# The last layer's softplus: second sum on VectorE, later steps, six buffers; first half part's sums copied by VectorE

## The chip, the cores and the metric

The kernel runs on one core of one Trainium2 chip. The metric is the time of one execution in device microseconds (us); the table below gives the median of three runs and one profiled execution. The engines are named as in the profile: PE (matmul) and PEld (its weight loads), DVE (VectorE), ACT (ScalarE), POOL (GpSimd), SP (the queue that issues most transfers).

## The reference, cut to what matters

Causal attention with a cumulative bias (2 batches, 8 heads, 576 tokens, head size 64) gives 1152 tokens of width 512. A mixture of eight experts follows, whose gate is normalised by rows and columns eight times. The last layer is a plain two-matmul block whose activation is softplus:

```python
def _moe2_ref(x, w_in, w_out) -> np.ndarray:
    h = x @ w_in                                     # 1152 x 512 by 512 x 2048
    g = np.maximum(h, 0.0) + np.log1p(np.exp(-np.abs(h)))
    return (g @ w_out).astype(np.float32)            # 1152 x 2048 by 2048 x 512
```

## The kernel before, in words

Attention comes first. Then 20 "half parts" `x` run one after the other, each with 512 columns of a hidden layer: 16 for the eight experts (`x < NX`, NX = 16), and four for the last layer (x = 16 to 19). Every float32 operand is split into its highest bits (`hh`, `w1h`, `xh`; type fp32r) and the rest (`hl`, `w1l`, `xl`), so that one product takes three matmuls.

Each half part has two stages of PE work, and the hand-written order mixes the second stage of one half part with the first stage of the next:

- First stage in the last layer, `plain` (line 340). A unit is 128 hidden columns by 288 tokens. It takes twelve matmuls into one bank `ph` and is played as two steps `p` of six matmuls. There are sixteen units for each half part, eight for tokens 0 to 575 (`g` = 0) and eight for tokens 576 to 1151 (`g` = 1).
- After each unit `evict` (line 230) makes softplus from the bank. ACT takes the absolute value, its exponential and log1p (lines 250 to 252, tiles `a1` and `a3`). `sums` puts four instructions into the queues: DVE computes 1 + a1 - 1 (line 256) and max(h, 0) + a3 (line 257), which is the bank's last reader; POOL computes a1 less that rounded value (line 258, into `a2`) and adds it to `a3` (line 259). `high` then rounds `a3` to `hh` on ACT (line 262), and `rest_` subtracts it on DVE, giving `hl` (line 265). The three tiles come from the pool `m3`, four buffers each.
- Second stage, `downs` (line 359). For a tile `t` of 128 tokens it adds four steps `d` of three matmuls into a bank `py`, which read `hh`, `hl` and the output weights `w2h`, `w2l`. After the fourth step `total` (line 382) takes the bank into `acc`: ACT copies it for the first half part of either layer (x = 0 and x = 16, line 385), and DVE adds it otherwise (line 388, or line 391 with the gate). There are two `py` banks, `y1` and `y2`, used in turn, so the first matmul of a tile waits for the `total` of the tile two before it.

The engines' queues keep the order in which the program issues instructions. `defer(k, step)` sets when a step is issued: `flush()` is called once for every `p` and every `d`, and a step deferred with `k` is issued at the flush numbered k + 1 after it. So `sums`, `high` and `rest_` are issued at flush 2, 5 and 6 after the unit's end. The order of the last layer's half parts is written out by hand, `=n` and `wn` starting the splitting of the next half part's weights (ACT line 146 and DVE line 149 for `w1`; ACT line 199 and DVE or POOL line 201 for `w2`):

```python
A_PLAIN = "p p p p d d p d p d p d p d =0 p d p d p d p d p d p d p d p =1 d d d"
B_PLAIN = "d d =2 d d p p d p d p d p p d p d p d p d p d p d d w0 p d d w2 p d d w1 p d d w3 p p"
A_GROUPS = [(0, 1), (2,), (3,)]
B_GROUPS = [(4,), (5,), (6,), (7, 8)]
```

In `A_PLAIN` the `p` steps are units of the same half part with `g` = 1 and the `d` steps are tiles 0 to 3 (tiles 0 and 1 share their steps, one matmul group each in turn). In `B_PLAIN` the `d` steps are tiles 4 to 8 and the `p` steps are units of the next half part with `g` = 0. Ahead of half part 16 twelve `p` follow each other with transposes of the layer's input (`turn`, lines 899 to 921) between them, and the four `p` of `A_PLAIN` follow on those. Half part 19 ends with twenty `d` alone.

Of the kernel before, what the change touches and what calls it, by code (L numbers as in the profile page):

```python
# [14 lines left out]
ALU = mybir.AluOpType  # L15
# [5 lines left out]
def attention_moe_ffn(ctx, tc, q, k, v, s, w_gate, w1, w2, w_in, w_out, out):  # L21
    nc = tc.nc
# [11 lines left out]
    NX = w1.shape[0]  # L34
# [18 lines left out]
    def f(ap):  # L53
        return ap.bitcast(F32)
# [154 lines left out]
    m3_t = []  # L209
# [4 lines left out]
    def defer(k, x):  # L214

        late.append([k, x])
# [13 lines left out]
    def evict(x, k, z, q, cols):  # L230

        hh, hl = hb[0][:, q, cols], hb[1][:, q, cols]
        if x < NX:
            def high():
                nc.scalar.activation(out=hh, in_=z, func=AF.Relu)  # L235

            def rest_():
                nc.vector.scalar_tensor_tensor(out=hl, in0=z, scalar=0.0, in1=f(hh), op0=ALU.max, op1=ALU.subtract)  # L238

            if k < 0:  # L240
                high()
            else:
                defer(k, high)
            defer(k + 1, rest_)
            return
        m3 = m3_t[-1]
        a1 = m3.tile([P, HB], F32, tag="a1", name="a1")
        a2 = m3.tile([P, HB], F32, tag="a2", name="a2")
        a3 = m3.tile([P, HB], F32, tag="a3", name="a3")
        nc.scalar.activation(out=a1, in_=z, func=AF.Abs)  # L250
        nc.scalar.activation(out=a1, in_=a1, func=AF.Exp, scale=-1.0)  # L251
        nc.scalar.activation(out=a3, in_=a1, func=AF.Ln, bias=1.0)

        def sums():

            nc.vector.tensor_scalar(a2, a1, 1.0, -1.0, ALU.add, ALU.add)  # L256
            nc.vector.scalar_tensor_tensor(out=a3, in0=z, scalar=0.0, in1=a3, op0=ALU.max, op1=ALU.add)
            nc.gpsimd.tensor_tensor(out=a2, in0=a1, in1=a2, op=ALU.subtract)  # L258
            nc.gpsimd.tensor_tensor(out=a3, in0=a3, in1=a2, op=ALU.add)  # L259

        def high():
            nc.scalar.activation(out=hh, in_=a3, func=AF.Copy)  # L262

        def rest_():
            nc.vector.tensor_tensor(out=hl, in0=a3, in1=f(hh), op=ALU.subtract)  # L265

        defer(1, sums)
        defer(4, high)
        defer(5, rest_)

    class Unit:

# [56 lines left out]
        def p3(self):  # L329
            self.product(self.a, S4, B22, False)  # L330
            flush()
            evict(self.x, -1, self.a, self.p, self.h1)
# [26 lines left out]
    def downs(x, groups):  # L359

        for tiles in groups:
            py = {}
            for t in tiles:
                nd[0] += 1
                py[t] = ps.tile([P, DM], F32, tag=f"y{1 + nd[0] % 2}", name="py", bufs=1)
            if x == XE:
                for t in tiles:
                    a = acc[0][:, t, :]
                    nc.gpsimd.tensor_scalar(a, a, gate_t[0][:, t, 0:1], 1.0, ALU.mult, ALU.mult)
            for k, ft in enumerate((0, 2, 1, 3)):  # L370
                wh, wl = wt[x, 2, ft]
                for t in tiles:
                    tsl = slice(t * P, (t + 1) * P)
                    hh, hl = hb[0][:, ft, tsl], hb[1][:, ft, tsl]
                    for n, (u, v) in enumerate(((hh, wh), (hh, wl), (hl, wh))):
                        nc.tensor.matmul(py[t], u, v, start=(k == 0 and n == 0), stop=(k == NF - 1 and n == 2))  # L376
                    flush()
                    if k == NF - 1:
                        total(x, t, py[t])
                    yield  # L380

    def total(x, t, py):
        a = acc[0][:, t, :]
        if x == 0 or x == NX:
            nc.scalar.activation(out=a, in_=py, func=AF.Copy)
            return
        if x < XE or x > NX:
            nc.vector.tensor_tensor(out=a, in0=py, in1=a, op=ALU.add)  # L388
        else:
            e = x // XE  # L390
            nc.vector.scalar_tensor_tensor(out=a, in0=py, scalar=gate_t[0][:, t, e:e + 1], in1=a,  # L391
                                           op0=ALU.mult, op1=ALU.add)
        if x == NH - 1:
            nc.sync.dma_start(out=out[t * P:(t + 1) * P, :], in_=a)
# [3 lines left out]
    with tc.manual_schedule():  # L398
# [500 lines left out]
        def turn(g):  # L899

            h, l = (z.rearrange("p b c n -> p b (c n)") for z in (xh[g], xl[g]))
            r = slice(g * REM, (g + 1) * REM)
            t0, o0 = (NB + 1, REM) if g else (0, 0)
            o1 = 0 if g else NB * P
            px = ps.tile([P, KD, REM], F32, tag="tr", name="px", bufs=2)
            for c in range(KD):
                nc.tensor.transpose(px[:, c, :], acc[0][r, NB, c * P:(c + 1) * P], ident[r, r])
            o = slice(o1, o1 + REM)
            nc.scalar.activation(out=h[:, :KD, o], in_=px, func=AF.Copy)
            yield  # L910
            nc.vector.tensor_tensor(out=l[:, :KD, o], in0=px, in1=f(h[:, :KD, o]), op=ALU.subtract)
            yield
            o = slice(o0, o0 + NB * P)
            for c in range(KD):
                px = ps.tile([P, 512], F32, tag="tr", name="px", bufs=2)
                for t in range(NB):
                    nc.tensor.transpose(px[:, t * P:(t + 1) * P], acc[0][:, t0 + t, c * P:(c + 1) * P], ident)
                nc.scalar.activation(out=h[:, c, o], in_=px, func=AF.Copy)
                yield
                nc.vector.tensor_tensor(out=l[:, c, o], in0=px, in1=f(h[:, c, o]), op=ALU.subtract)  # L920
                yield
# [23 lines left out]
        def rest():  # L945
            for z in back:
                for _ in z:
                    pass
            back.clear()
# [3 lines left out]
        def products(x, g):  # L953

            if x < NX:
                u = dict(a=Unit(x, 0, g), b=Unit(x, 1, g))
                return {z: getattr(u[z[0]], "p" + z[1]) for z in ORDER.split()}

            def sums():
                for i in range(2):  # L960
                    for j in range(2):
                        for p in range(2):
                            yield from plain(x, p, g, i, j)

            z = sums()
            return {"p": lambda: next(z)}

        def play(seq, todo, d=None):


            for z in seq.split():
                if z[0] in "=w":
                    dense[0] = z[0] == "w"
                if z[0] == "=":
                    back.append(prep1(x + 1, int(z[1])))
                    continue
                if z[0] == "w":
                    back.append(prep2(x + 1, int(z[1])))
                    continue
                if z == "d":  # L980
                    next(d)
                else:
                    todo[z]()
                step(z)
# [8 lines left out]
        x = -1  # L993
# [4 lines left out]
        for x in range(NH):  # L998
            if x == NX - 2:
                for _ in conv:  # L1000
                    pass
                cv.close()
                m3_t.append(ctx.enter_context(tc.tile_pool(name="m3", bufs=4, reuse_waits="tile")))
            play(A_SEQ if x < NX else A_PLAIN, products(x, 1), downs(x, A_GROUPS))
            d = downs(x, B_GROUPS if x + 1 < NH else [(t,) for t in range(NB, NTT)])
            if x + 1 < NX:
                play(B_SEQ, products(x + 1, 0), d)
            elif x + 1 == NX:
                play("d d d d", {}, d)
                rest()  # L1010
                back.append(turn(0))
                for _ in range(8):
                    play("d", {}, d)
                    step()
                rest()
                u = products(NX, 0)
                play("d d w0 p d d w2 p d d w1 p d d w3 p", u, d)
                back.append(turn(1))
                play("p p p p p p p p p p p p", u)
                rest()  # L1020
            elif x + 1 < NH:
                play(B_PLAIN, products(x + 1, 0), d)
            else:
                play(" ".join("d" * 20), {}, d)
            if x == XE - 1:
                for _ in gates:
                    pass
                gt.close()
                conv = convert(cv.enter_context(tc.tile_pool(name="cv", bufs=2, reuse_waits="tile")))
# [56 lines left out]
```

## Time and profile before

| what | value |
|---|---|
| median of three runs | 1121.05 us (1119.55 to 1121.26) |
| the profiled execution's own time | 1118.75 us |
| span of the profile, first to last instruction | 1117.0 us |
| mean granted TensorE clock | 0.991 of full speed |
| busy: PE, PEld, DVE, ACT, POOL | 1080.4, 951.8, 737.8, 528.1, 419.6 us |

The profile shows one execution. The last layer's units begin about 891 us into the span and its last matmul starts at 1112.50 us. PE is busy for 97% of the whole span, so what other engines do matters only where PE stands still or runs at a lower clock.

### The profile page before, as it was taken

Reading aid. Unit: us, or ns where it says so; the run is one execution under the profiler, and the core shown is the slowest. Engines: PE = TensorE matmul, PEld = TensorE weight load, DVE = VectorE, ACT = ScalarE, POOL = GpSimd, SP = SyncE. Lnnn points to the kernel's source line nnn. Section 1 sums busy time; section 2 is a strip of 40 time slices with the busy share of each in tenths; the row PEclk is TensorE's granted clock in tenths of the full one; section 3 lists DMA queues with packets and bytes.
Section 4 is the critical chain, followed back from the end, with each engine's and each line's share of the span. In section 5 each row is a group of like instructions: output and inputs, shape, how many; then the busy total and the mean of one; then the engine's idle time right before and its main releaser. Section 6 shows DMA issues by size and latency. Waiting matters only on the chain.

```text
span 1117.0 us, 18144 instructions
## 1 busy us (share of the span) xinstructions
PE 1080.4 (97%) x6692; PEld 951.8 (85%) x6692; DVE 737.8 (66%) x1641; ACT 528.1 (47%) x1246; POOL 419.6 (38%) x493
## 2 busy tenths in 40 slices
PE   4989999999999999999999999999999999999998
PEld 3767789898988988889888898889889898888887
DVE  4456645847878778787878888775555575465553
ACT  3988644233443434334343443334334267656551
POOL 5876411134423324142341523413020065555552
PEclk9999999999999999999999999999999999999999
DMA  5222102032122322223132222311112111111001
GB/s 171 85 78 66 40 1 76 3 112 94 67 94 95 125 83 87 95 94 121 60 114 95 95 90 75 129 58 38 38 39 76 38 39 38 39 38 38 1 11 75
DMA packets 30424, 78.48 MB, mean 70 GB/s; under 512 B 6048, under 2 KB 10656, under 8 KB 30336
## 3 DMA queue, kind: packets, MB, share of 16 engines
q1 hardware_dynamic: 27768, 68.93, 19.1%
q0 software_dynamic: 2560, 8.39, 1.9%
q8 instruction: 52, 0.85, 0.3%
q14 instruction: 36, 0.29, 0.1%
q10 hardware_dynamic: 8, 0.01, 0.0%
HBM read 66.00 MB, written 10.82 MB: 69 GB/s over the span
## 4 chain that ended last, share of the span: by engine, by line
PE 82%; DVE 7%; ACT 5%; POOL 3%; issue 2%; SPq 1%; DMA 0%; POOLq 0%; DVEq 0%; ACTq 0%
PE py L376 41%; PE ph L287 31%; PE ph L351 4%; POOL a L259 2%; PE sc L551 1%; POOL a L258 1%; PE pv L665 1%; DVE a L256 1%; DVE hl L265 1%; PE tr L639 1%; ACT hh L262 1%; ACT a L251 1%; ACT eb L608 1%; PE tr L633 1%; ACT a L250 1%
## 5 line engine op out<-in xcount | busy, mean ns | idle before, releaser
L376 PE MATMUL py<-w2h,hh 128*128 128x512 f32 x720 | 287.2, 399 | 7.4 <-DVE acc L388 6.1
L376 PE MATMUL py<-w2h,hl 128*128 128x512 f32 x720 | 285.2, 396 | 1.0 <-DVE hl L238 1.0
L376 PE MATMUL py<-w2l,hh 128*128 128x512 f32 x720 | 285.2, 396 | 0.0
L287 PE MATMUL ph<-xh,w1h 128*128 128x288 f32 x896 | 265.1, 296 | 2.5 <-ACT v L295 2.5
L287 PE MATMUL ph<-xh,w1l 128*128 128x288 f32 x896 | 264.8, 296 | 0.0
L287 PE MATMUL ph<-xl,w1h 128*128 128x288 f32 x896 | 263.3, 294 | 0.0
L287 PEld LDWEIGHTS ph<-xh,w1h 128*128 128x128 f32 x896 | 167.9, 187 | 20.0 <-ACT v L295 2.8
L287 PEld LDWEIGHTS ph<-xl,w1h 128*128 128x128 f32 x896 | 168.3, 188 | 16.5
L287 PEld LDWEIGHTS ph<-xh,w1l 128*128 128x128 f32 x896 | 168.2, 188 | 0.0
L376 PEld LDWEIGHTS py<-w2h,hl 128*128 128x128 f32 x720 | 135.7, 188 | 34.1 <-DVE hl L238 1.6
L201 POOL TENSOR_TENSOR w2l<-raw,w2h 128x512 fp32r<-128x512 f32 x40 | 55.4, 1384 | 287.4 <-ACT w2h L199 287.4
L235 ACT ACTIVATE hh<-ph 128x288 fp32r<-128x288 f32 x192 | 78.8, 412 | 159.8 <-DVE ph L337 81.2
L376 PEld LDWEIGHTS py<-w2h,hh 128*128 128x128 f32 x720 | 135.5, 188 | 21.2 <-DVE acc L388 6.8
L376 PEld LDWEIGHTS py<-w2l,hh 128*128 128x128 f32 x720 | 135.9, 189 | 11.6
L295 ACT ACTIVATE v<-ph 128x288 f32<-128x288 f32 x128 | 51.0, 411 | 171.7 <-PE ph L287 164.8
L391 DVE SCALAR_TENSOR_TENSOR acc<-py,gate,acc 128x512 f32<-128x512 f32 x126 | 94.0, 746 | 54.2 <-PE py L376 54.0
L894 POOL TENSOR_TENSOR cm<-cm,ct 128x512 f32<-128x512 f32 x32 | 45.1, 1409 | 202.5 <-DVE ct L892 202.5
L238 DVE SCALAR_TENSOR_TENSOR hl<-ph,hh 128x288 fp32r<-128x288 f32 x192 | 86.7, 454 | 30.5 <-ACT hh L235 28.7
L149 DVE TENSOR_TENSOR w1l<-raw,w1h 128x512 fp32r<-128x512 f32 (+1 forms) x144 | 99.8, 694 | 8.3 <-ACT w1h L146 8.2
L265 DVE TENSOR_TENSOR hl<-a,hh 128x288 fp32r<-128x288 f32 x64 | 38.0, 594 | 71.9 <-ACT hh L262 71.9
L146 ACT ACTIVATE w1h<-raw 128x512 fp32r<-128x512 f32 (+1 forms) x144 | 82.9, 577 | 1.6 <-PE ph L287 1.6
L258 POOL TENSOR_TENSOR a<-a,a 128x288 f32<-128x288 f32 x64 | 51.8, 809 | 78.8 <-DVE a L256 61.4
(182 smaller groups left out, 1766.1 us busy)
## 6 DMA issues: line engine op xcount, KB each, us to landing
raw<-in_w SPq DMA_DIRECT2D x64, 512.0 KB
f<-in_w_in SPq DMA_DIRECT2D x16, 512.0 KB
f<-in_w_out SPq DMA_DIRECT2D x16, 512.0 KB
wd<-cm POOLq DMA_DIRECT2D x32, 256.0 KB, 3.2
raw<-wd SPq DMA_DIRECT2D x16, 512.0 KB
out<-acc SPq DMA_DIRECT2D x9, 256.0 KB
vv<-in_v SPq DMA_DIRECT2D x8, 256.0 KB
qk<-in_k SPq DMA_DIRECT2D x7, 288.0 KB
```

Of the source, the lines that this page charges most:

```text
L146: nc.scalar.activation(out=hi[:, o], in_=t[:, src], func=AF.Copy)
L149: nc.vector.tensor_tensor(out=lo[:, o], in0=t[:, src], in1=f(hi[:, o]), op=ALU.subtract)
L201: (nc.gpsimd if i else nc.vector).tensor_tensor(out=lo, in0=t[:, r], in1=f(hi), op=ALU.subtract)
L235: nc.scalar.activation(out=hh, in_=z, func=AF.Relu)
L238: nc.vector.scalar_tensor_tensor(out=hl, in0=z, scalar=0.0, in1=f(hh), op0=ALU.max, op1=ALU.subtract)
L258: nc.gpsimd.tensor_tensor(out=a2, in0=a1, in1=a2, op=ALU.subtract)
L265: nc.vector.tensor_tensor(out=hl, in0=a3, in1=f(hh), op=ALU.subtract)
L287: nc.tensor.matmul(o, u, v, start=(start and c == 0 and n == 0), stop=(c == 1 and n == 2), skip_group_check=True)
L295: nc.scalar.activation(out=t, in_=self.a, func=AF.Copy)
L376: nc.tensor.matmul(py[t], u, v, start=(k == 0 and n == 0), stop=(k == NF - 1 and n == 2))
L391: nc.vector.scalar_tensor_tensor(out=a, in0=py, scalar=gate_t[0][:, t, e:e + 1], in1=a, op0=ALU.mult, op1=ALU.add)
L894: nc.gpsimd.tensor_tensor(out=m, in0=m, in1=f(t), op=ALU.add)
```

## The change

In the last layer the addition of line 259 leaves POOL: it becomes a step of its own, `total_`, on DVE, deferred by 3 (flush 4). `high` is deferred by 5 instead of 4 (flush 6) and `rest_` by 7 instead of 5 (flush 8). The pool `m3` has six buffers for each tile instead of four. In `total`, the nine copies of half part 16 go from ACT (an activation) to DVE (`tensor_copy`); half part 0 keeps ACT.

```diff
@@ evict
             nc.gpsimd.tensor_tensor(out=a2, in0=a1, in1=a2, op=ALU.subtract)
-            nc.gpsimd.tensor_tensor(out=a3, in0=a3, in1=a2, op=ALU.add)
+
+        def total_():
+            nc.vector.tensor_tensor(out=a3, in0=a3, in1=a2, op=ALU.add)
...
         defer(1, sums)
-        defer(4, high)
-        defer(5, rest_)
+        defer(3, total_)
+        defer(5, high)
+        defer(7, rest_)
@@ total
-        if x == 0 or x == NX:
+        if x == 0:
             nc.scalar.activation(out=a, in_=py, func=AF.Copy)
             return
+        if x == NX:
+            nc.vector.tensor_copy(a, py)
+            return
@@ x == NX - 2
-                m3_t.append(ctx.enter_context(tc.tile_pool(name="m3", bufs=4, reuse_waits="tile")))
+                m3_t.append(ctx.enter_context(tc.tile_pool(name="m3", bufs=6, reuse_waits="tile")))
```

## Rows read from the trace of the kernel before

**Rows 1.** The waits from 890 us to the end: waiter, releaser, us in total, times, longest.
```profile
DVE hl L265 <- ACT hh L262: 71.9, 51, 2.9
POOL a L258 <- DVE a L256: 61.4, 45, 3.3
ACT hh L262 <- POOL a L259: 56.7, 44, 2.9
...
PE py L376 <- DVE acc L388: 6.1, 3, 2.1
...
PE py L376 <- ACT acc L385: 1.0, 1, 1.0
...
PE ph L351 <- DVE xl L920: 0.5, 1, 0.5
```

**Rows 2.** PE's timeline: start, us, instruction, idle before it and its releaser.
```profile
925.57 0.29 PE L351 MATMUL ph<-xh,w1l 128*128 128x288 f32 x1
926.89 0.50 PE L376 MATMUL py<-w2h,hh 128*128 128x512 f32 x1 [1.03 <-ACT acc L385]
...
954.16 0.40 PE L376 MATMUL py<-w2h,hl 128*128 128x512 f32 x1
954.66 0.50 PE L376 MATMUL py<-w2h,hh 128*128 128x512 f32 x1
...
975.45 0.40 PE L376 MATMUL py<-w2h,hl 128*128 128x512 f32 x1
...
977.85 0.29 PE L351 MATMUL ph<-xh,w1l 128*128 128x288 f32 x1
980.11 0.50 PE L376 MATMUL py<-w2h,hh 128*128 128x512 f32 x1 [1.97 <-DVE acc L388]
```

**Rows 3.** DVE's timeline ahead of the release at 980 us.
```profile
978.41 0.46 DVE L265 TENSOR_TENSOR hl<-a,hh 128x288 fp32r<-128x288 f32 x1 [1.66 <-ACT hh L262]
...
979.01 0.45 DVE L257 SCALAR_TENSOR_TENSOR a<-ph,a 128x288 f32<-128x288 f32 x1
979.37 0.68 DVE L388 TENSOR_TENSOR acc<-py,acc 128x512 f32<-128x512 f32 x1
```

**Rows 4.** The chain that ended last, after two stalls: start, us, what.
```profile
980.11 0.96 PE py L376 x3
981.07 0.79 PE ph L351 x6
981.87 0.69 PE py L376 x3
...
1033.03 1.65 PE py L376 x3
1034.68 1.44 PE ph L351 x6
1036.12 0.90 PE py L376 x3
```

**Rows 5.** Stretches: us, busy (x count) of PE, PEld, DVE, ACT, POOL; clock, DMA.
```profile
897.00:927.00 30.00, 28.50 (x194) 26.53 (x193) 23.00 (x42) 21.48 (x53) 21.24 (x25) 1.00 0.10 36
...
1088.00:1097.00 9.00, 9.00 (x47) 8.16 (x46) 3.88 (x11) 3.89 (x10) 4.12 (x6) 0.83 0.23 87
```

**Rows 6.** Single lines from 890 us: count, least/median/largest duration in ns, first and last start.
```profile
L252 ACT ACTIVATE a<-a x64: 444/447/449, 895.5 to 1097.8; 128x288 f32<-128x288 f32 x64
...
L256 DVE TENSOR_SCALAR a<-a x64: 298/304/920, 895.5 to 1099.0; 128x288 f32<-128x288 f32 x64
L257 DVE SCALAR_TENSOR_TENSOR a<-ph,a x64: 444/452/460, 895.9 to 1099.2; 128x288 f32<-128x288 f32 x64
L258 POOL TENSOR_TENSOR a<-a,a x64: 795/808/822, 897.8 to 1099.4; 128x288 f32<-128x288 f32 x64
L265 DVE TENSOR_TENSOR hl<-a,hh x64: 443/459/1072, 900.3 to 1101.6; 128x288 fp32r<-128x288 f32 x64
L388 DVE TENSOR_TENSOR acc<-py,acc x27: 677/687/692, 979.4 to 1112.9; 128x512 f32<-128x512 f32 x27
```

## The prediction, made before the change was run

> **What bounds the kernel now.** I read first the share of each engine: PE is busy for 97% of the span, so only what stops or slows PE counts. The change touches half parts 16 to 19 alone, some 225 us. The view of waits for that stretch [rows 1] shows that PE stands still for others only three times for line 388, 6.1 us together, once for line 385, 1.0 us, and 0.5 us for the split input `xl`. The long rows above those are not PE's: DVE waits 71.9 us for `hh`, ACT 56.7 us for POOL's second addition, POOL 61.4 us for DVE's line 256. Read together they are one ring: `hl` of a unit blocks DVE's queue until ACT has rounded, ACT's until POOL has added, and POOL gets nothing from the next unit until DVE is free.
>
> PE's timeline says where this ring reaches PE [rows 2]: at 926.89 and 980.11, and in the same place of `A_PLAIN` in the two half parts after them, always at the first matmul of tile 2. It needs the bank of tile 0. Tile 0's last matmul at 975.45 ends at 975.85, but DVE takes that bank only at 979.37 [rows 3], 3.5 us later. In front of it stands an `hl` that sat idle for 1.66 us, and `sums` of the next unit. So the stall is order on DVE, not work: between 897 and 927 us, its fullest stretch, DVE is busy 23.00 of 30 us [rows 5].
>
> The chain that ended last gives a second cost [rows 4]. After the stall at 980 us two tiles' steps and a unit's step take 0.96 + 0.79 + 0.69 = 2.44 us. After the next one the same three take 1.65 + 1.44 + 0.90 = 3.99 us, and a ph matmul takes just under twice its time: the lower of the two clock levels, 1.2 GHz instead of 2.4. The last stall is followed by the same pattern, and the stretch from 1088 to 1097 us has a granted clock of 0.83 [rows 5]. It came after idle of about 2.06 us (twice), not after 1.97 or 1.03 us.
>
> **The change part by part.** *Later `hl` and `hh`.* A unit in the mixed stretches of `A_PLAIN` takes PE two `p` and two `d`, 2 x 0.79 + 2 x 0.69 = 2.96 us [rows 4], and four flushes. `hl` is now issued two flushes later, 1.5 us, `hh` one. When DVE comes to `hl` of a unit, its second sum has been issued four flushes, some 3 us, before, so the head-of-queue wait for `hh` should go. Then the bank of tile 0 is taken when its last matmul ends. Ahead of `total` stands then `sums` of the unit that ended some 2.2 us earlier (d, p, d); ACT's three activations need 3 x 0.45 us from its end, as line 252, and line 257 another 0.45 [rows 6], 1.8 together, so DVE is free at about the time the matmul ends. The release is due 0.69 us after 975.85 [rows 2, 6], at 976.5, and the bank is wanted at 977.98: 1.4 us to spare. So all four stalls go. Their price: 6.1 + 1.0 = 7.1 us idle [rows 1], and with the start-up of the pipe 2.26 us from start to start instead of 0.13 at 980, which is 0.16 more than its 1.97 idle [rows 2]; times four, 0.6. Together 7.7 us. With them goes what is late at the lower clock: 3.99 - 2.44 = 1.55 us, twice, 3.1 us [rows 4].
>
> *The second sum on DVE.* 64 additions of the form of line 265, so 0.46 us each alone and 1.07 beside POOL at worst [rows 6]: 29 to 69 us of DVE in a stretch where it idles nearly half the time. POOL loses 64 instructions of the length of line 258, 52 us. DVE per unit: 0.30 + 0.45 + 0.46 + 0.46 = 1.67 us, and if the whole of POOL's 0.81 us blocks it, 2.48 us, under 2.96. I take no cost: PE's 2.96 us hides it. The new sum waits on DVE for POOL's line 258, which starts after line 256; 257 lies between, so at most 0.81 - 0.45 = 0.4 us of a unit, where the old wait was 71.9 / 51 = 1.4 us. Where POOL has a weight subtraction of 512 columns in front (line 201, twice for each half part), by the same length for each column 0.81 x 512 / 288 = 1.4 us (an estimate), it is up to 1.8 us; those come at the end of `B_PLAIN`, well ahead of the bank that the stalls wait for. Queued behind it on DVE are `sums` and `total`; who waits for those are PE (bank) and POOL.
>
> On this place the Trainium skill (SBUF — State Buffer, "Who interferes with whom") says that a VectorE instruction with two inputs in SBUF and a GpSimd instruction that reads SBUF exclude each other, the first one in keeping the port to its end. The trace agrees: line 265 spreads from 443 to 1072 ns while line 257, which reads a bank, stays within 444 to 460 [rows 6]. By that rule moving an addition to VectorE adds an instruction that can be shut out, which speaks against the change; it also removes half of what shuts out.
>
> *The nine copies of half part 16.* DVE takes some 0.69 us each, as line 388 [rows 6]. They no longer stand behind `hh` in ACT's queue: the 1.0 us at 926 is already counted, and PE's start at 954.66, 0.50 us after the last one instead of 0.23, lost another 0.3 [rows 2]. Six us more on DVE over 60 us is covered by its idle time.
>
> *Six buffers.* Between a unit's activations and its `hl` lie eight flushes; in the run of sixteen `p` those are four units, so four buffers would block ACT there and six do not. No wait of before is for these buffers, so this gains nothing by itself.
>
> *The run of sixteen `p`.* There ACT, DVE and POOL are near their limit [rows 5]: 21.48, 23.00, 21.24 of 30 us busy. In the DVE-POOL ring a unit costs before 0.30 + 0.81 + 0.81 + 0.46 = 2.4 us of excluding work, afterwards 0.30 + 0.81 + 0.46 + 0.46 = 2.0 [rows 6]. The 0.5 us that PE waits for `xl` [rows 1] may go or stay, since ACT is as busy as ever: 0 to 0.5, I take half, 0.25.
>
> *New small waits.* Not shown by this trace; from nothing to the like of the 0.3 us at 954. I take 0.3 once.
>
> Sum: 7.7 + 3.1 + 0.3 + 0.25 - 0.3 = 11.0 us. The profiled execution took 1118.75 us for a span of 1117.0, 2.3 under the median of 1121.05; I take the gain off the median: **1110.0 us**, -1.0%.
>
> **The rivals.**
> (a) *The wait only moves.* DVE's queue has a new instruction at whose head it waits for POOL, so part of the lateness stays: the stalls shrink by a third to two thirds, and the clock may still fall once. For it: POOL still answers 0.81 us after line 256. Against: 0.4 us a unit against 1.4. Gain 3 to 8 us, middle 5.5: 1115.5 us.
> (b) *Nothing changes*, because the bank comes late for another reason, say ACT's queue holding line 252 back. For it: ACT waits as well [rows 1]. Against: its wait is for the addition that leaves POOL. 1121 us.
> (c) *Slower: `hl` comes too late.* After its later issue PE has 3.8 us until it reads it at the tightest place (the second pair of `d` after the sixteen `p`) and 4.2 us at four others (the first tile of `B_PLAIN`, thrice, and tile 6 of half part 19), by counting steps at 0.79 and 0.69; before it was 5.4 to 5.7. It decides once DVE runs more than 3.8 us behind PE; before, it was 3.5 late [rows 2, 3], with waits that should go. With the stalls kept and about 1 us lost at five places, and 1.55 us of clock at two, 1121 + 8 = 1129 us.
> (d) *Slower: DVE becomes the bound.* If each of the four instructions of a unit took its longest, 0.92 + 0.46 + 1.07 + 1.07 = 3.5 us [rows 6], it would pass PE's 2.96 and lose 0.55 us on 64 units, 35 us, less the 11: 1145 us. It decides from 2.96 us on. Against: POOL has only 0.81 us a unit with which to shut it out, which gives 2.48. The rule on the port named above would be its cause; by that same rule each exclusion lasts no longer than POOL's instruction.
>
> **How the numbers follow.** Forecast 0.75, its own range 1107.5 to 1113.5: all that is named, 7.7 + 3.1 + 0.3 + 0.5 = 11.6, and 1.9 for scatter such as the runs of before show (1119.55 to 1121.26) below; one of the two slow-clock stretches and half a stall left, 3 us, above. (a) 0.14, (b) 0.05, (c) and (d) 0.03 each. The range that holds 8 in 10 takes the lower half of (a) with it: 1107.5 to 1115.5. A measurement of this kernel can tell about 0.2%, 2.2 us. Faster by more: 0.75 + 0.14 = 0.89; within: 0.05; slower: 0.06.
>
> **What would show it.** Right: no PE wait for a `total` at the first matmul of tile 2; DVE's wait for `hh` from 71.9 to under 15 us; a DVE wait for line 258 in its place, under 35 us; the granted clock at 1.00 from 897 us to the last matmul; a span of about 1106. Wrong: PE waiting for `hl` or `hh`; DVE busy through a stretch while PE waits; the lower clock appearing again after a shorter pause; a new PE wait for a `ph` bank, which would mean that line 257 came later.

## The result, and the profile after

| | before | after |
|---|---|---|
| median of four runs | 1120.86 us (1119.55 to 1121.26) | 1107.38 us (1107.13 to 1108.78) |
| ratio | | 0.9884, 95% interval 0.9867 to 0.9901 |
| span of the profiled execution | 1117.0 us | 1107.0 us |
| first matmul of half part 16's units to the last matmul | 891.36 to 1112.50: 221.14 us | 893.78 to 1102.60: 208.82 us |

The change makes the kernel 1.2% faster. The last row of the table is the measure used below: it begins where the changed part begins. Ahead of it the profiled execution after was 2.4 us later than that of before, in work that the change does not touch; inside it, it is 12.3 us shorter.

Line numbers after: the second sum is line 261, `hh` 264, `hl` 267; the units' matmuls 354, the tiles' matmuls 379, the copies 391, the additions 394. First the view of waits, from 890 us to the end (waiter, releaser, us, times, longest):

```profile
POOL a L258 <- DVE a L256: 124.1, 61, 5.7
...
ACT hh L264 <- DVE a L261: 28.5, 26, 2.9
DVE a L256 <- ACT a L251: 15.7, 15, 2.5
...
DVE acc L394 <- PE py L379: 12.6, 13, 2.1
DVE a L261 <- POOL a L258: 7.2, 11, 2.2
```

No row of PE is left in this view, where before there were 7.6 us [rows 1]. DVE's 71.9 us for `hh` are gone altogether; `hl` finds it ready every time. What takes its place on DVE is 7.2 us for POOL's line 258. ACT still waits for the second sum in front of `hh`, 28.5 us where it was 56.7 [rows 1]. POOL waits most, and nobody waits for POOL for long.

PE's timeline at the first matmul of tile 2 of half part 17, and DVE's ahead of it (start, us, instruction):

```profile
977.84 0.29 PE L354 MATMUL ph<-xh,w1l 128*128 128x288 f32 x1
977.96 0.40 PE L379 MATMUL py<-w2h,hh 128*128 128x512 f32 x1
```
```profile
975.96 0.45 DVE L257 SCALAR_TENSOR_TENSOR a<-ph,a 128x288 f32<-128x288 f32 x1
976.33 0.68 DVE L394 TENSOR_TENSOR acc<-py,acc 128x512 f32<-128x512 f32 x1
```

From start to start it is now 0.12 us, where it was 2.26 [rows 2]. DVE takes tile 0's bank at 976.33 and frees it at 977.01, 0.95 us before it is wanted; there is no idle time in front of it, so `sums` of the unit before, which ends at 976.41, still sets when it starts. The stretches (us, busy time of PE, PEld, DVE, ACT, POOL with counts, clock, DMA) show the rest:

```profile
897.00:927.00 30.00, 30.00 (x204) 28.19 (x203) 24.76 (x57) 23.84 (x58) 12.22 (x14) 1.00 0.11 36
...
1060.00:1088.00 28.00, 28.00 (x171) 25.49 (x170) 23.54 (x48) 17.12 (x43) 10.81 (x12) 1.00 0.08 29
1088.00:1102.80 14.80, 14.80 (x65) 11.71 (x63) 5.24 (x10) 1.14 (x3) 0.81 (x1) 1.00 0.23 89
```

PE is busy without a break, and the granted clock is 1.00 where it was 0.83 [rows 5]. DVE is busy 24.76 of 30 us in the fullest stretch, only 1.8 us more than before although it has a dozen additions more; line 256 alone takes 3.6 us of this stretch (12 times) where it took 7.1 (11 times). The single lines (count, least, median and largest ns) show where that went:

```profile
L256 DVE TENSOR_SCALAR a<-a x64: 292/301/313, 897.9 to 1087.9; 128x288 f32<-128x288 f32 x64
L261 DVE TENSOR_TENSOR a<-a,a x64: 443/448/1548, 901.0 to 1090.0; 128x288 f32<-128x288 f32 x64
L267 DVE TENSOR_TENSOR hl<-a,hh x64: 443/726/1014, 903.3 to 1092.4; 128x288 fp32r<-128x288 f32 x64
```

Line 256, up to 0.92 us before [rows 6], is never held up now: by the timelines POOL stands idle while it runs, in 63 cases of 64. `hl` now often meets POOL at work, and its median rises from 0.46 to 0.73 us; the 35 of the 64 that take over 0.6 us all overlap an instruction of POOL.

### The profile page after: what moved, and what is told of

Read it like the earlier page. It is cut to its first block, busy times and chain, and to the rows that moved or that the text cites. A ratio compares the mean times of both kernels' runs of the same rounds, so it can differ in the third digit from the quotient of the medians.

```text
span 1107.0 us, 18106 instructions
## 1 busy us (share of the span) xinstructions
PE 1078.4 (97%) x6692; PEld 950.8 (86%) x6692; DVE 770.2 (70%) x1714; ACT 522.1 (47%) x1237; POOL 363.0 (33%) x429
## 4 chain that ended last, share of the span: by engine, by line
PE 92%; DVE 3%; ACT 1%; issue 1%; SPq 1%; DMA 0%; POOL 0%; DVEq 0%; ACTq 0%; POOLq 0%
PE py L379 45%; PE ph L290 32%; PE ph L354 9%; PE sc L557 2%; PE pv L671 1%; PE tr L645 1%; PE tr L639 1%; DMA raw<-in_w 0%; PE sc L561 0%; PE pg L817 0%; ACT eb L614 0%; DVE xl L88 0%; ACT xh L85 0%; PE pv L681 0%; DVE w1l L149 0%
## 5 line engine op out<-in xcount | busy, mean ns | idle before, releaser
L290 PE MATMUL ph<-xh,w1h 128*128 128x288 f32 x896 | 265.5, 296 | 2.5 <-ACT v L298 2.5
L379 PEld LDWEIGHTS py<-w2l,hh 128*128 128x128 f32 x720 | 135.3, 188 | 11.7
L354 PE MATMUL ph<-xh,w1h 128*128 128x288 f32 x256 | 76.0, 297 | 0.0
```

Source lines behind the costliest of these rows:

```text
L290: nc.tensor.matmul(o, u, v, start=(start and c == 0 and n == 0), stop=(c == 1 and n == 2), skip_group_check=True)
L354: nc.tensor.matmul(o, u, v, start=(n == 0), stop=(n == 11))
```

## The experiments

Two theories stood against each other. A: what cost time was order, `hl` standing at the head of DVE's queue with `hh` not there. B: what cost time was work, POOL's second addition, by its length in the chain and by shutting DVE out while it runs. "Stretch" is the measure of the table above; each ratio is against runs of the kernel before on the same chip (median 1119.46 us for the first four experiments, 1119.47 for the others).

| kernel | median, us | ratio, 95% interval | stretch, us | PE's waits in it, us |
|---|---|---|---|---|
| before (profile) | 1120.86 | 1 | 221.14 | 0.47, 1.03, 1.97, 2.06, 2.06 |
| e1_later_only | 1109.03 | 0.9902 (0.9888 to 0.9916) | 209.56 | 0.29 |
| e2_sum_only | 1113.87 | 0.9945 (0.9931 to 0.9959) | 214.61 | 1.30, 1.70, 1.72 |
| e3_copy_only | 1120.66 | 1.0008 (0.9997 to 1.0018) | 221.70 | 0.47, 1.70, 2.31, 2.07, 2.00 |
| e5_copies_on_act | 1108.64 | 0.9898 (0.9884 to 0.9912) | 208.90 | none |
| e4_four_buffers | 1107.43 | 0.9885 (0.9867 to 0.9902) | 208.83 | none |
| e7_hl_only | 1110.24 | 0.9915 (0.9898 to 0.9932) | 211.58 | 0.31, 0.94 |
| e9_hl_flush12 | 1108.13 | 0.9894 (0.9877 to 0.9910) | 209.98 | 0.89 |
| e6_stalls | 1117.58, one run | | 222.33 | 1.78, 3.22, 5.39 |
| after (profile) | 1107.38 | 0.9884 (0.9867 to 0.9901) | 208.82 | none |

**Only the later steps** (e1_later_only), on the kernel before:

```diff
-        defer(4, high)
-        defer(5, rest_)
+        defer(5, high)
+        defer(7, rest_)
...  m3: bufs=4 -> bufs=6
```

> Only the later steps and the six buffers: both additions stay on POOL, the nine copies stay on ACT. Theory A (order: what cost time was hl standing at the head of DVE's queue while hh was not there): the stalls at the first matmul of tile 2 go in half parts 17 to 19, DVE's wait for hh falls from 71.9 us to under 15, and nearly the whole gain is there, 10 to 13 us less than before. Theory B (work and length: what cost time was POOL's second addition, in the chain and at the port that it shares with DVE): the chain is as long and POOL as busy as before, so the bank still comes late; less than 4 us of gain.

The stretch falls by 11.6 of the 12.3 us, the time by 1.0%. DVE's wait for `hh` goes from 71.9 to 7.3 us although the chain is as long as before and both additions are on POOL. Its rows in the view of waits:

```profile
POOL a L258 <- DVE a L256: 63.2, 50, 4.8
...
ACT hh L262 <- POOL a L259: 23.8, 25, 2.9
...
DVE hl L265 <- ACT hh L262: 7.3, 10, 1.2
```

Theory A holds.

**Only the second sum on DVE** (e2_sum_only), on the kernel before:

```diff
-            nc.gpsimd.tensor_tensor(out=a3, in0=a3, in1=a2, op=ALU.add)
+        def total_():
+            nc.vector.tensor_tensor(out=a3, in0=a3, in1=a2, op=ALU.add)
...
+        defer(3, total_)
         defer(4, high)
         defer(5, rest_)
```

> Only the second addition on DVE (issued at flush 4); hh and hl at flush 5 and 6, four buffers and the copies on ACT as before. Theory A: hl still stands before sums of the next unit and waits for hh, which stands behind the next unit's three activations on ACT; the ring is shorter by some 0.4 us (0.81 on POOL against 0.45 on DVE), so the stalls shrink and do not all go: DVE's wait for hh stays above 30 us, gain 3 to 8 us. Theory B: the gain is here, 10 to 13 us, with no PE wait for a bank.

About half the gain: 6.5 us of the stretch, 0.55% of the time. DVE's wait for `hh` falls to 25.9 us, less than the 30 expected. Three bank stalls remain, shorter; the one of half part 16 and the wait for `xl` are gone. DVE's timeline ahead of the release at 978.94 us:

```profile
977.24 0.46 DVE L267 TENSOR_TENSOR hl<-a,hh 128x288 fp32r<-128x288 f32 x1 [0.51 <-ACT hh L264]
977.62 0.30 DVE L256 TENSOR_SCALAR a<-a 128x288 f32<-128x288 f32 x1
977.84 0.45 DVE L257 SCALAR_TENSOR_TENSOR a<-ph,a 128x288 f32<-128x288 f32 x1
978.20 0.68 DVE L391 TENSOR_TENSOR acc<-py,acc 128x512 f32<-128x512 f32 x1
```

It is the picture of [rows 3] with a wait of 0.51 us instead of 1.66: the ring is shorter, and still a ring. Of the 6.5 us some 3.0 are the two clock falls that the shorter stalls did not bring.

**Only the copies on DVE** (e3_copy_only), on the kernel before:

```diff
-        if x == 0 or x == NX:
+        if x == 0:
             nc.scalar.activation(out=a, in_=py, func=AF.Copy)
             return
+        if x == NX:
+            nc.vector.tensor_copy(a, py)
+            return
```

> Only the nine copies of half part 16 on DVE. Theory A: DVE is blocked by hl there as in the other half parts, so the copy comes as late as line 388 does and the stall of 1.0 us at 926 grows to about 2; same time or 1 us more. Theory B (ACT's queue was what made that one late): the stall of 1.0 us and the 0.3 us at 954 go, 1 to 1.5 us less.

Nothing is gained: 1.0008 (0.9997 to 1.0018) cannot be told from no change. The 0.3 us at 954 go, as theory B had it, but the stall of half part 16 grows from 1.03 to 1.70 us. DVE's timeline says why: the copy stands behind `hl` and `sums`, as line 388 does in the other half parts.

```profile
926.52 0.46 DVE L265 TENSOR_TENSOR hl<-a,hh 128x288 fp32r<-128x288 f32 x1 [1.66 <-ACT hh L262]
926.90 0.30 DVE L256 TENSOR_SCALAR a<-a 128x288 f32<-128x288 f32 x1
927.12 0.45 DVE L257 SCALAR_TENSOR_TENSOR a<-ph,a 128x288 f32<-128x288 f32 x1
927.49 0.68 DVE L388 COPY acc<-py 128x512 f32<-128x512 f32 x1
```

**The change without the copies** (e5_copies_on_act): the diff above taken back from the changed kernel.

> The changed kernel with the nine copies of half part 16 back on ACT. Theory A: with the ring gone ACT's queue is no longer late either, the time stays within 0.7 us of the changed kernel's 1107.4. Theory B: ACT still waits for the second sum before hh (up to 2.9 us in the trace after), so the copy is late at tile 2 and at tile 8: 1 to 2 us more than the changed kernel.

The stretch is 208.90 us against 208.82 and PE waits nowhere, which is theory A. The median, 1108.64, is 1.2 us above the changed kernel's, outside the 0.7 of theory A and as much as theory B expected; the two intervals of the table overlap, and the trace shows no late copy, so the 1.2 us are not traced to the copies. In the stretch that the change touches the copies may stand on either engine once the ring is gone.

**Four buffers** (e4_four_buffers), on the changed kernel:

```diff
-  m3: bufs=6
+  m3: bufs=4
```

> The changed kernel with four buffers in m3 instead of six. Theory A (the deferral needs the buffers): in the run of sixteen p log1p of a unit (line 252) has to wait until hl of the unit four before it is done, ACT shows waits for line 267 there, and since the bank's last reader follows on line 252, PE's wait for xl comes back; 0.5 to 2 us more than the changed kernel. Rival: DVE is never that late, ACT shows no such wait, and the time is the changed kernel's within 0.5 us.

208.83 us and no PE wait: the rival holds in the time. ACT does wait for `hl` at line 252, but the row of that line's idle time (us, times) is small:

```profile
  DVE hl L267: 0.6, 2
```

Six buffers bring nothing here; the prediction's sentence that four would block ACT in the run of sixteen `p` is true of 0.6 us which PE never sees.

**`hl` alone** (e7_hl_only), on the kernel before: `hl` at flush 8 and six buffers; `hh` and all else in place.

```diff
-        defer(5, rest_)
+        defer(7, rest_)
...  m3: bufs=4 -> bufs=6
```

> The kernel before with hl alone later (flush 8 instead of 6) and six buffers; hh stays at flush 5, both additions on POOL, the copies on ACT. Theory A: hl at the head of DVE's queue was the link that closed the ring, so this one number takes most of the gain: as with hh later too, 9 to 12 us less than before, DVE's wait for hh under 15 us. Rival: hh at flush 5 still blocks ACT until POOL's second addition is done, sums of the next unit comes late by that, and half the stalls stay: 3 to 7 us less.

The stretch falls by 9.6 of the 12.3 us. The three stalls for line 388 are gone, DVE's wait for `hh` is 6.6 us. The six buffers came with it; that they bring nothing was shown on the changed kernel (e4) and not on this one. What stays is where ACT's queue is still held by `hh`: the copy of half part 16 on ACT comes late by nearly as much as before.

```profile
ACT hh L262 <- POOL a L259: 39.3, 36, 2.9
```
```profile
926.14 0.51 PE L376 MATMUL py<-w2h,hh 128*128 128x512 f32 x1 [0.94 <-ACT acc L385]
```

**Later still** (e9_hl_flush12), on the changed kernel:

```diff
-        defer(7, rest_)
+        defer(11, rest_)
```

> The changed kernel with hl later still: issued at flush 12 instead of 8, some 3 us. By counting steps 0.8 us are left until PE reads it at one place and 1.2 us at four others, less than the 0.5 to 1 us that DVE takes for the instruction and those ahead of it, or about as much. Theory A (the rival of the prediction in which hl comes too late, with its place): PE waits for hl at those places, 0.3 to 2 us each, 2 to 7 us more than the changed kernel. Rival: DVE has caught up at those places and PE waits nowhere, the same time within 0.7 us.

One of the five places gives way, the tightest: the second pair of `d` after the sixteen `p`. PE's timeline there, and DVE's:

```profile
917.72 0.40 PE L379 MATMUL py<-w2l,hh 128*128 128x512 f32 x1
919.00 0.50 PE L379 MATMUL py<-w2h,hl 128*128 128x512 f32 x1 [0.89 <-DVE hl L267]
```
```profile
917.98 0.96 DVE L267 TENSOR_TENSOR hl<-a,hh 128x288 fp32r<-128x288 f32 x1
```

The stretch grows by 1.2 us, less than the 2 to 7 expected. At the four places with 1.2 us by count DVE is in time. The medians, 1108.13 and 1107.38, do not separate the two kernels; the trace does.

**Added stalls** (e6_stalls), on the changed kernel; `junk` is read by nothing:

```diff
+        if x > NX:
+            for _ in range({(NX + 1, 0): 4, (NX + 2, 0): 6, (NX + 3, 0): 9}.get((x, t), 0)):
+                nc.vector.tensor_reduce(junk[0][:, 0:1], py, AX.X, ALU.max)
```

> The changed kernel with 4, 6 and 9 additional reductions of the bank ahead of the first total (tile 0) of half parts 17, 18 and 19, whose result nothing reads, so that DVE frees the bank late by 0.6 us for each. With some 0.9 us to spare PE should stand still there for about 1.5, 2.7 and 4.5 us. Theory A: a late bank costs its idle time and 0.25 us of start-up, and when TensorE's clock falls to its lower level after it, 1.5 us more whatever the length; from the kernel before (a fall after 2.06 us twice, none after 1.03 and 1.97) the clock falls after the second and third: 8.7 + 0.75 + 3.0 = 12.5 us more from the first unit's matmul of half part 16 to the last matmul than the 208.8 us of the changed kernel. Rival 1: the clock's loss grows with the length of the stall. Rival 2: the clock falls have nothing to do with these stalls, and none appears: 9.5 us more.

The three stalls are 1.78, 3.22 and 5.39 us, since a reduction took 0.70 us and not 0.6. The chain after each (start, us, what):

```profile
974.19 0.96 PE py L380 x3
975.15 0.79 PE ph L355 x6
...
1028.07 1.52 PE py L380 x3
1029.59 1.44 PE ph L355 x6
1031.03 1.03 PE py L380 x3
...
1085.68 1.65 PE py L380 x3
1087.33 1.44 PE ph L355 x6
1088.77 1.17 PE py L380 x3
```

After 1.78 us of idle the clock stays up; after 3.22 and 5.39 it falls, with ph matmuls at the length of [rows 4], and three pieces take 3.99 and 4.26 us instead of the 2.44 of [rows 4]: 1.55 and 1.82 us lost. So the loss hardly grows with the stall, and rivals 1 and 2 fall, on one execution. Idle and clock together are 10.4 + 3.4 = 13.8 us; the stretch is 13.5 us longer.

## Why the prediction was right, and where it was not

The mechanism is as predicted, and e1, e2 and e7 show it: `hl` at the head of DVE's queue made the banks late. POOL's addition made the wait longer (e2), but with both additions left on POOL no bank is late (e1). All four bank stalls went, with the two clock falls behind them, so the two large terms, 7.7 and 3.1 us, stand.

The size was short: 11.0 us against 12.3 in the stretch and 13.5 between the medians (11.1 to 14.9 by the interval); 1107.38 us lies 0.1 under the stated range. The terms that were mis-sized are the small ones. The wait for `xl` went wholly (0.5 instead of 0.25, 0.6 from start to start), the new small wait of 0.3 us did not come, and the slower first matmuls after a stall (0.50 us instead of 0.40, [rows 2]) were left out. With them the sum is 7.7 + 3.1 + 0.3 + 0.6 = 11.7 us, and 12.3 with that last 0.1 us at each of six restarts (near 912, 926, 954, 980, 1033 and 1087 us). The other 1.2 us between the medians is not in the stretch: e4, with the same stretch, came out 12.0 us below its own runs of before.

By steps:

- *The bank of tile 0, 1.4 us to spare.* It is 0.95: released at 977.01 instead of 976.5, since `sums` of the unit before ended at 976.4 and not at about 975.9. ACT was done with that unit's line 252 at 975.32; what DVE still had in front of `sums` was an `hl` of 0.98 us from 974.47, with POOL's line 258 running beside it, and a second sum of 0.45, and the prediction put nothing there.
- *No cost for 64 additions on DVE.* Right in the sum, but the worst case was set too low. Line 261 took up to 1.55 us, not 1.07. DVE's row and POOL's at that place:

```profile
960.55 1.54 DVE L261 TENSOR_TENSOR a<-a,a 128x288 f32<-128x288 f32 x1
```
```profile
960.27 1.50 POOL L201 TENSOR_TENSOR w2l<-raw,w2h 128x512 fp32r<-128x512 f32 x1
```

  The addition starts 0.28 us into a weight subtraction of POOL and ends 0.32 us after it. This is the exclusion of the Trainium skill (SBUF — State Buffer, "Who interferes with whom"), and the trace agrees. ACT's longest wait for the second sum is at the same place: `hh` of that unit waited 2.87 us, of which this exclusion makes some 1.1 (1.54 less the 0.45 of an undisturbed one).
- *Rival (a), the wait only moves.* It did not: DVE's 71.9 us for `hh` became 7.2 us for line 258, and ACT's 56.7 us for the second sum became 28.5. What is left of them costs PE nothing; no row of PE is in the view.
- *Rival (b), ACT's queue makes the banks late.* Not in half parts 17 to 19: in e7 ACT still waits 39.3 us for POOL's addition, and the three stalls are gone. In half part 16, where ACT itself frees the bank, it does.
- *Rival (c), `hl` too late.* It did not come. Issued three microseconds later still (e9), `hl` shows that the place was right and the count of places and the price were not: one place of five gave way, for 0.9 us.
- *Rival (d), DVE becomes the bound.* It does not: DVE is busy 24.76 of 30 us at the fullest, and PE never waits for it.
- *The copies.* The 1.0 us at 926 was put down to ACT's queue. True of the kernel before, but the cure was not the move: alone it makes the stall longer (e3), and without it the stretch is as short (e5).
- *The six buffers* gain nothing, as said; nor are they needed: with four ACT is blocked for 0.6 us in all (e4).

Taken one at a time, the later steps give 11.6 us of the stretch and the second sum 6.5, and they are mostly the same microseconds: on top of the later steps, the sum and the copies together are worth 0.7, nearly all of it the wait for `xl`, of which e1 keeps 0.29 us.

## What to carry to other kernels

Where PE waits for an engine that is busy half of the time, look at what stands at the head of that engine's queue, and whose result it wants; issuing that instruction later in program order can be a small edit; here it was one number, with room in the buffers. How late it can go is to be counted in steps of the bounding engine from its issue to its reader, with room for the engine's own lag: here 3.8 us at the tightest place was enough and 0.8 was not. An instruction moved to an engine that is itself blocked gains only what it takes out of the ring: the nine copies on DVE alone gained nothing (e3), the second sum, which made the ring shorter, about half (e2).

## What the runs showed of the hardware

Whether TensorE's clock falls after a pause is not told by the pause's length alone. In these profiles the granted clock stayed at its upper level (2.4 GHz) after pauses of 1.03, 1.30, 1.70 (twice), 1.72, 1.78, 1.97 and 2.31 us, and fell to the lower (1.2 GHz) after 2.00, 2.06 (twice), 2.07, 3.22 and 5.39 us. The 2.31 and the 2.07 are in one execution, e3_copy_only; its chain after each:

```profile
981.41 0.95 PE py L376 x3
982.36 0.79 PE ph L351 x6
```
```profile
1034.32 1.47 PE py L376 x3
1035.78 1.44 PE ph L351 x6
```

After the pause of 2.00 us, in the same execution, the first matmul still took 0.50 us and the two behind it 0.56 and 0.63: the clock fell after PE had started again. Each fall cost 1.5 to 1.8 us, whatever the pause. The Trainium skill (TensorE: Matmul & The Clock Gate, "What's actually happening") says that the chip's observation of TensorE runs freely and is not reset by the kernel, so that the moment of a change depends on where it happens to stand; it says so of the rise after a kernel's first matmuls. The falls above agree with that and do not prove it; what decides between 2.31 and 2.00 us stays open.
